# Linear attention and a mixture of experts on one core: the scanned decays go through DRAM, and 17 sets of prepared buffers become 19

## The chip, the core and the metric

The kernel runs on one core of a Trainium2 chip. A core has five engines that run side by side: TensorE (PE, matrix products, with a row of its own for weight loads, PEld), VectorE (DVE), ScalarE (ACT), GpSimd (POOL) and SyncE (SP, which here only issues transfers). Each works through its own list of instructions in order and waits where one needs a result that is not there yet; an instruction behind a waiting one waits too. Transfers are carried by 16 DMA engines that all issuing engines share. The metric is the device time of one execution in microseconds (us), less is better.

## The reference

Two computations follow each other, all in 32-bit floats. The first is a recurrence over 768 tokens for 4 batches and 8 heads of width 40:

```python
for t in range(S):
    y[:, :, t] = einsum('bhd,bhde->bhe', r_t, state)
    Sa = einsum('bhde,bhe->bhd', state, a_t)
    state = state * w_t[:, :, None, :] - einsum('bhd,bhe->bhde', Sa, b_t) + einsum('bhd,bhe->bhde', v_t, k_t)
```

The second takes the 3072 outputs `y` as rows of 320, forms gate logits `x @ w_gate`, balances their exponentials over rows and experts in 8 rounds, and sums over 8 experts `P[:, e] * (relu(x @ w1[e]) @ w2[e])`, with a hidden width of 1024.

## The kernel before

**The recurrence** is done in 12 chunks of 64 tokens (`c`), each for 4 batches (`b`): 48 steps in all, in the order of `c`, then `b`. Within a chunk the products of decays `w` are folded into `k`, `b`, `a` and the output, so that a chunk becomes a handful of small matrix products and the inverse of a triangular matrix. Three kinds of work make it up.

- A **preparation** (`prep`, lines 112 to 171, one for each `c, b`) needs only inputs. It loads them in one transfer (`inp`, line 115, 522 KB), scans the decays twice on VectorE (`q`, line 120, and `g`, line 128), multiplies `k` and `b` by `q` (`kb`, line 139) and `a` by `g` (`ab`, lines 145 and 146) on GpSimd, and forms four products `ll` and four transposes `kt` on TensorE (lines 151 and 159). What it leaves for the step later is a **set** of buffers: `sx`, `bb`, `cc` and `g`. There are `NSX` = 17 sets, used in rotation, so preparation n can write its set only when step n-17 is done with it. One part of `ll` goes to DRAM (`ld`, lines 154 and 170).
- An **inversion** (one for each pair of chunks, a segment, so six of them) starts when the eight preparations of the segment are done. It loads what they stored (`load_lu`, line 369), works on VectorE in 15 stages (`inv_diag`, `contract`, lines 173 to 223, about 24 us of VectorE time), ends with the copy `tn` (line 358), and stores two halves `ud` and `nd` to DRAM (lines 360 and 361). `tload` (lines 225 to 244) loads them back in another layout (`td`, `tt`), and `tmat` (lines 246 to 260: products `gp` and `op` on TensorE with copies on ScalarE between) makes of them the matrices `tt` of a chunk.
- A **step** (`recur`, lines 262 to 329) loads `v`, `r` and `vt` (lines 265 to 269), runs `av`, `xc`, `pu` (line 297, with `tt`) and `c2` on TensorE with masks and copies between them, adds up `ws` on VectorE, multiplies by `g` on GpSimd for the output `y` (line 308), stores `y` as `xd` (line 312), and hands the state `z` on. A step needs the state of the same batch one chunk before, so four of them overlap. Its gate products `lp` (line 334) follow a few steps later.

The program is written as a list of events with due times (lines 385 to 409): step (c, b) is due at 5c + 1.1b, preparation n just after step n - `NSX` at the earliest (line 399), an inversion after the last preparation of its segment. A scheduler then orders each engine's instructions by its own estimate of when they could run, with that list as priority. So `NSX` decides where preparations, and with them the inversions, stand among the steps.

**Memory.** The sets lie in pools of their own, in the order of last use (lines 33 and 50 to 63), and the second part's buffers (`stg`, `x0`, `hp`, `x1`, lines 477 to 495) take over their addresses when the first part lets go of them. Eight of the sets (`IN_SETS` and `KB_SETS`) are one raw tile, which the first preparations use for other things before it is a set.

**The experts** (lines 497 to 714) are split into 128 blocks; from block 8 the order of the work is written out by hand. Weights are loaded and split into a high and a low part on GpSimd and ScalarE ahead of use (`prep_w`, lines 497 to 528).

Of the kernel before, what the change touches and what calls it, by code (L numbers as in the profile page):

```python
# [11 lines left out]
F32 = mybir.dt.float32  # L12
F32R = mybir.dt.float32r
AF = mybir.ActivationFunctionType
ALU = mybir.AluOpType
# [5 lines left out]
NP = 4  # L21
R2 = 104
# [6 lines left out]
def attention(ctx, tc, d, xd, ps, pq, pt, gs, lg):  # L29
    nc = tc.nc  # L30
    pin = ctx.enter_context(tc.tile_pool(name="a_in", bufs=1))
    inv = ctx.enter_context(tc.tile_pool(name="a_inv", bufs=1))
    sets = [ctx.enter_context(tc.tile_pool(name=f"a_set{i}", bufs=1)) for i in range(NSX)]
    const = ctx.enter_context(tc.tile_pool(name="a_const", bufs=1))
    io = ctx.enter_context(tc.tile_pool(name="a_io", bufs=1))
    wk = ctx.enter_context(tc.tile_pool(name="a_wk", bufs=2))
    dr = ctx.enter_context(tc.tile_pool(name="a_dr", bufs=2, space=bass.MemoryType.DRAM))
# [7 lines left out]
    one65 = cst[0:R2, 400:660]  # L45

    NTB = 2
    sx_b, bb_b, g_b, cc_b = ([None] * NSX for _ in range(4))
    raws = {}
    for n in range(NCH * NB - NSX, NCH * NB):  # L50
        i, pool = n % NSX, sets[n - NCH * NB + NSX]
        if i in IN_SETS or i in KB_SETS:
            raw = pool.tile([128, 1508], F32, name=f"st{i}")
            raws[i] = raw
            sx_b[i] = raw[0:R2, 0:832].rearrange("r (p h x) -> r p h x", h=2, x=104)
            bb_b[i] = raw[:, 832:1248].rearrange("r (p x) -> r p x", x=104)
            g_b[i] = raw[0:R2, 1248:1504].rearrange("r (p x) -> r p x", x=64)
            cc_b[i] = raw[0:R2, 1504:1508]
            continue
        sx_b[i] = pool.tile([R2, NP, 2, 104], F32, name=f"sx{i}")  # L60
        bb_b[i] = pool.tile([128, NP, 104], F32, name=f"bb{i}")
        g_b[i] = pool.tile([R2, NP, 64], F32, name=f"g{i}")
        cc_b[i] = pool.tile([R2, NP], F32, name=f"cc{i}")
    tt_b = [const.tile([128, 4 * NP, 128], F32, name=f"tt{i}") for i in range(NTB)]
    td_b = [const.tile([128, 4 * NP, 32], F32, name="td")]
# [20 lines left out]
    def clear():  # L86
# [5 lines left out]
        for t in tt_b:  # L92
            nc.gpsimd.memset(t, 0.0)
    fresh = set(range(NSX))

    def first_use(i):
        if i in fresh:
            fresh.discard(i)
            nc.gpsimd.memset(bb_b[i], 0.0)
            nc.scalar.copy(out=sx_b[i][64:R2].rearrange("r p h x -> r (p h) x")[:, :, 64:104],  # L100
                           in_=cst[64:R2, 360:400].unsqueeze(1).broadcast_to([40, 8, 40]))
# [3 lines left out]
    def rot(key, lst):  # L105
        i = state[key]
        state[key] = (i + 1) % len(lst)
        return lst[i]
# [3 lines left out]
    def prep(c, b, ld):  # L112
        cb = c * NB + b
        inp = raws[IN_MAP[cb]][0:R2, 0:1284] if IN_MAP.get(cb) else pin.tile([R2, 1284], F32, name="inp", bufs=2)
        nc.sync.dma_start(out=inp, in_=d["inp"][c, b])
        w65 = inp[:, 0:516]
        kb_in = inp[:, 516:1028].rearrange("r (p k t) -> r p k t", p=NP, k=2)
        a_in = inp[:, 1028:1284].rearrange("r (p t) -> r p t", p=NP)
        q = pin.tile([R2, NP, 65], F32, name="q")
        nc.vector.tensor_tensor_scan(  # L120
            out=q.rearrange("r p t -> r (p t)"), data0=w65[:, 0:260], data1=one65,
            initial=0.0, op0=ALU.mult, op1=ALU.add)
        g1 = rot("g1", g1_b)
        nc.vector.reciprocal(out=g1[:, :, 0], in_=q[:, :, 64])
        sx = rot("sx", sx_b)
        i = next(j for j in range(NSX) if sx_b[j] is sx)
        g, bb, cc = g_b[i], bb_b[i], cc_b[i]
        nc.vector.tensor_tensor_scan(
            out=g.rearrange("r p t -> r (p t)"), data0=w65[:, 260:516],
            data1=g1.rearrange("r p t -> r (p t)"), initial=0.0, op0=ALU.mult, op1=ALU.add)  # L130
        if cb < NKB:
            raw = raws[KB_SETS[cb % len(KB_SETS)]]
            kb = raw[0:R2, 0:512].rearrange("r (p k t) -> r p k t", p=NP, k=2)
            lt = raw[0:64, 512:1024].rearrange("r (p k t) -> r p k t", p=NP, k=2)
        else:
            kb = pin.tile([R2, NP, 2, 64], F32, name="kb")
            lt = pin.tile([64, NP, 2, 64], F32, name="lt")
        eng = nc.vector if cb < NFAST else nc.gpsimd
        (nc.gpsimd if cb in KB_POOL else eng).tensor_tensor(
            out=kb, in0=kb_in,  # L140
            in1=q[:, :, 63::-1].unsqueeze(2).broadcast_to([R2, NP, 2, 64]), op=ALU.mult)
        ab = rot("ab", ab_b)
        first_use(i)
        nc.gpsimd.tensor_copy(out=cc, in_=q[:, :, 64])
        eng.tensor_tensor(out=ab[0:40, :, 0:64], in0=a_in[0:40], in1=g[0:40], op=ALU.mult)
        eng.tensor_tensor(out=ab[64:104, :, 64:128], in0=a_in[64:104], in1=g[64:104], op=ALU.mult)  # L146
        nc.scalar.copy(out=sx[64:104, :, 0, 0:64], in_=ab[0:40, :, 0:64])
        nc.scalar.copy(out=sx[64:104, :, 1, 0:64], in_=ab[64:104, :, 64:128])
        ll = pq.tile([128, NP, 2, 64], F32, name="ll", tag="pq")
        for p in range(NP):  # L150
            nc.tensor.matmul(ll[:, p], lhsT=kb[:, p], rhs=ab[:, p], start=True, stop=True)  # L151
        if cb < NKB:
            nc.scalar.activation(out=lt, in_=ll[64:128], func=AF.Copy, scale=-1.0)
            (nc.sync if cb < N_SP else nc.scalar).dma_start(out=ld[GRP[c][1], :, b], in_=lt)
            kt = pt.tile([128, NP, 2, 64], F32, name="kt", tag="pt")
        else:
            kt = pq.tile([128, NP, 2, 64], F32, name="kt", tag="pq")
        for p in range(NP):
            nc.tensor.transpose(kt[:, p].rearrange("s h x -> s (h x)")[:, 0:R2],
                                kb[:, p].rearrange("r k s -> r (k s)"), ident[0:R2, 0:R2])  # L160
        nc.vector.tensor_tensor(
            out=sx[0:64, :, :, 0:64], in0=ll[0:64],
            in1=mask_u.unsqueeze(1).unsqueeze(1).broadcast_to([64, NP, 2, 64]), op=ALU.mult)
        if cb >= NKB:
            nc.scalar.activation(out=lt, in_=ll[64:128], func=AF.Copy, scale=-1.0)
        nc.scalar.copy(out=sx[0:64, :, :, 64:104], in_=kt[0:64, :, :, 0:40])
        nc.scalar.activation(out=bb[0:64, :, 0:40], in_=kt[64:128, :, 0, 0:40], func=AF.Copy, scale=-1.0)
        nc.scalar.activation(out=bb[64:128, :, 64:104], in_=kt[64:128, :, 1, 0:40], func=AF.Copy, scale=-1.0)
        if cb >= NKB:
            (nc.sync if cb < N_SP else nc.scalar).dma_start(out=ld[GRP[c][1], :, b], in_=lt)  # L170
        return dict(cc=cc, g=g, sx=sx, bb=bb)

    def inv_diag(us, i):
        nu = us.stop - us.start
# [87 lines left out]
    def recur(c, b):  # L262
        pp = preps[c, b]
        vz, zc = vz_cur[b], zp[b]
        nc.sync.dma_start(out=vz[:, :, 0:64], in_=d["v"][c, b])
        rb = io.tile([R2, NP, 128], F32, name="rb", bufs=NRB)
        nc.sync.dma_start(out=rb, in_=d["r"][c, b])
        f = wk.tile([R2, NP, 2, 104], F32, name="f", bufs=NFB)
        nc.sync.dma_start(out=f[0:64].rearrange("s p h x -> s (p h) x")[:, :, 64:104],
                          in_=d["vt"][c, b].rearrange("s (g x) -> s g x", x=40))  # L270
# [6 lines left out]
        for p in range(NP):  # L277
            nc.tensor.matmul(av[:, p], lhsT=vz[:, p], rhs=rb[:, p], start=True, stop=True)  # L278
        nc.vector.tensor_tensor(
            out=f[:, :, :, 0:64], in0=av,  # L280
            in1=mask_f.unsqueeze(1).unsqueeze(1).broadcast_to([R2, NP, 2, 64]), op=ALU.mult)
# [14 lines left out]
        for p in range(NP):  # L296
# [3 lines left out]
                                op=ALU.mult)  # L300
# [4 lines left out]
        ws = wk.tile([R2, NP, 104], F32, name="ws")  # L305
        nc.vector.tensor_tensor(out=ws, in0=c2, in1=c1, op=ALU.add)
        y = wk.tile([R2, NP, 64], F32, name="y", bufs=NY)
        nc.gpsimd.tensor_tensor(out=y, in0=ws[:, :, 0:64], in1=pp["g"], op=ALU.mult)
        col = (b % 2) * 192 + (c % 3) * 64
        tok = (c // 3) * 768 + (col // 128) * 256 + (b // 2) * 128 + col % 128  # L310
        for h in range(2):
            nc.sync.dma_start(
                out=xd[h * 160:h * 160 + 160].rearrange("(p e) t -> e p t", e=40)[:, :, tok:tok + 64],
                in_=y[h * 64:h * 64 + 40])
        gq.append(gate(c, b, y))
        if c + 1 == NCH:
# [3 lines left out]
                                in1=preps[c + 1, b]["cc"].unsqueeze(2).broadcast_to([R2, NP, 40]), op=ALU.mult)  # L320
# [54 lines left out]
    def step(c, b):  # L375
        if (c, b) not in gens:
            gens[c, b] = recur(c, b)
        next(gens[c, b], None)

    def do_prep(s, c, b, first):  # L380
        if first:
            start_seg(s)
        preps[c, b] = prep(c, b, invs[s][0])
# [9 lines left out]
    for s, cs in enumerate(GROUPS):  # L393
# [3 lines left out]
        for i in range(n):  # L397
            cb = (cs[0] + i // NB, i % NB)
# [19 lines left out]
PD = 0.75  # L418
INV_DT = 0.05
SKEW = 1.1  # L420
NSX = 17
GL = 3
NY = 4
NFB = 3
# [2 lines left out]
IN_SETS = (16, 15, 14, 13)  # L427
# [409 lines left out]
```

## Time and profile before

| | us |
|---|---|
| median of 3 timed runs (lowest to highest) | 1893.79 (1890.14 to 1895.72) |
| the profiled execution's own time | 1882.69 |
| its span, first to last instruction | 1880.9 |
| TensorE busy, share of the span | 1774.0, 94% |
| mean granted TensorE clock | 0.945 |
| first `pu` of a step, last `pu` of a step | 108.58, 546.98 |

The profile is of one execution; times within it count from its first instruction. The recurrence fills roughly the first 555 us, the experts the rest, and they overlap a little at the seam. "Granted clock" is the share of full TensorE speed that the chip allowed at the time; read in windows of 10 us it lies between 0.50 and 1.00. "[4.47 <-DMA td<-nd]" behind a row means that the engine sat idle for 4.47 us before it and that this transfer ended the wait.

### The profile page before, as it was taken

The page shows a single profiled execution, that of the slowest core. Times are in us where ns is not written, and L with a number is a line of the kernel's source. Part 1 is how long each engine was busy: PE and PEld are TensorE (multiplying, and loading weights), DVE is VectorE, ACT ScalarE, POOL GpSimd, SP SyncE. Part 2 cuts the span into 40 slices and gives each one's busy share as a digit, 9 for nine tenths or more (in the row PEclk, how much of TensorE's full clock was granted, in tenths as well). Part 3 has the DMA queues.
Part 4 walks back from the last instruction along what each step waited for, and adds up shares of the span by engine and source line. Part 5 has one row for each costly group of instructions (what it writes and reads, how often), then busy time and mean ns, then how long its engine had stood idle before and what let it go on. Part 6 is the DMA issues. An engine that isn't in the chain of part 4 may idle for free.

```text
span 1880.9 us, 31865 instructions
## 1 busy us (share of the span) xinstructions
PE 1774.0 (94%) x12035; PEld 1733.0 (92%) x12035; DVE 1365.8 (73%) x2378; ACT 854.6 (45%) x1845; POOL 867.8 (46%) x846
## 2 busy tenths in 40 slices
PE   4489998899898999999999999999999999999999
PEld 4378887899788899999999999999999999999999
DVE  7865867848558867776777767886776867777676
ACT  6356667466543434343443434445343433434342
POOL 6545546331444345281744628004471826537170
PEclk8579989789689999999999999999999999999999
DMA  7578776685621111020111102111110201111011
GB/s 192 114 152 175 149 174 158 120 140 109 168 67 46 37 37 55 20 74 18 57 37 37 56 19 74 55 33 37 37 55 19 73 19 55 37 37 59 16 37 43
DMA packets 187839, 136.27 MB, mean 72 GB/s; under 512 B 155941, under 2 KB 165285, under 8 KB 187685
## 3 DMA queue, kind: packets, MB, share of 16 engines
q1 hardware_dynamic: 184485, 128.98, 27.7%
q10 hardware_dynamic: 3200, 5.25, 1.1%
q8 instruction: 95, 1.56, 0.4%
q14 instruction: 59, 0.48, 0.1%
HBM read 113.74 MB, written 20.45 MB: 71 GB/s over the span
## 4 chain that ended last, share of the span: by engine, by line
PE 78%; DVE 7%; DMA 7%; POOL 3%; issue 2%; ACT 2%; SPq 1%; ACTq 0%; POOLq 0%; DVEq 0%
PE op L637 35%; PE p L572 32%; DMA inp<-in_inp_dram 3%; PE xc L286 2%; PE pu L297 1%; PE ll L151 1%; PE av L278 1%; PE c L304 1%; PE lp L334 1%; DMA nd<-tn 1%; PE gp L253 1%; DVE pr L185 1%; DMA rb<-in_r_dram 1%; PE op L258 1%; POOL ab L146 1%
## 5 line engine op out<-in xcount | busy, mean ns | idle before, releaser
L572 PE MATMUL p<-xch,wh 128*128 128x384 f32 (+1 forms) x1792 | 605.6, 339 | 6.9 <-DVE u L590 2.4
L593 ACT ACTIVATE hh<-sm 128x384 fp32r<-128x384 f32 x512 | 269.4, 526 | 722.9 <-DVE sm L590 722.9
L637 PE MATMUL op<-wh,hh 128*128 128x320 f32 x1536 | 477.8, 312 | 2.9 <-ACT hh L593 2.8
L637 PE MATMUL op<-wl,hh 128*128 128x320 f32 x1536 | 475.6, 310 | 0.0
L637 PE MATMUL op<-wh,hl 128*128 128x320 f32 x1536 | 468.8, 311 | 2.4 <-DVE hl L596 2.4
L518 POOL TENSOR_TENSOR wl<-ws,wh 128x640 fp32r<-128x640 f32 x60 | 103.3, 1721 | 608.7 <-ACT wh L516 608.5
L596 DVE SCALAR_TENSOR_TENSOR hl<-sm,hh 128x384 fp32r<-128x384 f32 x512 | 368.0, 752 | 2.2 <-ACT hh L593 2.0
L572 PEld LDWEIGHTS p<-xch,wh 128*128 128x128 f32 (+1 forms) x1792 | 337.8, 189 | 10.4 <-DVE u L590 4.1
L572 PE MATMUL p<-xcl,wh 128*128 128x384 f32 x896 | 302.9, 338 | 0.0
L572 PE MATMUL p<-xch,wl 128*128 128x384 f32 x896 | 302.3, 337 | 0.0
L637 PEld LDWEIGHTS op<-wh,hh 128*128 128x128 f32 x1536 | 291.1, 189 | 3.7 <-ACT hh L593 3.7
L637 PEld LDWEIGHTS op<-wl,hh 128*128 128x128 f32 x1536 | 291.6, 190 | 0.0
L637 PEld LDWEIGHTS op<-wh,hl 128*128 128x128 f32 x1536 | 287.6, 188 | 3.2 <-DVE hl L596 3.1
L590 DVE TENSOR_TENSOR sm<-p,u 128x384 f32<-128x384 f32 x384 | 234.8, 621 | 8.8
L572 PEld LDWEIGHTS p<-xcl,wh 128*128 128x128 f32 x896 | 168.9, 188 | 0.0
L572 PEld LDWEIGHTS p<-xch,wl 128*128 128x128 f32 x896 | 168.8, 188 | 0.0
L590 DVE TENSOR_TENSOR sm<-p,p 128x384 f32<-128x384 f32 x128 | 71.3, 557 | 129.7 <-PE p L572 76.9
L590 DVE TENSOR_TENSOR p<-p,p 128x384 f32<-128x384 f32 x128 | 71.2, 556 | 103.6 <-PE p L572 101.6
L590 DVE TENSOR_TENSOR u<-p,p 128x384 f32<-128x384 f32 x128 | 70.8, 553 | 59.8 <-PE p L572 58.7
L526 POOL TENSOR_TENSOR wl<-ss,wh 128x512 fp32r<-128x512 f32 x60 | 90.8, 1514 | 35.3 <-ACT wh L523 31.2
L151 PE MATMUL ll<-ab,kb 104*128 104x128 f32 x336 | 63.7, 349 | 45.9 <-POOL ab L146 21.8
L151 PEld LDWEIGHTS ll<-ab,kb 104*128 104x128 f32 x336 | 55.5, 250 | 50.7 <-POOL ab L146 30.2
(166 smaller groups left out, 2793.9 us busy)
## 6 DMA issues: line engine op xcount, KB each, us to landing
ws<-in_wts_dram SPq DMA_DIRECT2D x60, 832.0 KB
inp<-in_inp_dram SPq DMA_DIRECT2D x42, 521.6 KB
rb<-in_r_dram SPq DMA_DIRECT2D x48, 208.0 KB
ld<-lt ACTq DMA_DIRECT2D x40, 128.0 KB
vz<-in_v_dram SPq DMA_DIRECT2D x48, 104.0 KB
f<-in_vt_dram SPq DMA_DIRECT2D x48, 80.0 KB
xd<-y SPq DMA_DIRECT2D x96, 40.0 KB
st<-in_inp_dram SPq DMA_DIRECT2D x6, 521.6 KB
```

The source lines that it names most:

```text
L146: eng.tensor_tensor(out=ab[64:104, :, 64:128], in0=a_in[64:104], in1=g[64:104], op=ALU.mult)
L151: nc.tensor.matmul(ll[:, p], lhsT=kb[:, p], rhs=ab[:, p], start=True, stop=True)
L185: nc.vector.tensor_tensor(out=prv, in0=a.unsqueeze(2).broadcast_to([nu, n_c, n_r, n_k]), in1=m.unsqueeze(1).broadcast_to([nu, n_c, n_r, n_ ...
L253: nc.tensor.matmul(gp[:, p], lhsT=lb[:, p], rhs=t1[:, p], start=True, stop=True)
L286: nc.tensor.matmul(xc[h][:, p], lhsT=pp["sx"][:, p, h], rhs=f[:, p, h], start=True, stop=True)
L518: g.tensor_tensor(out=wl[:, 0:640], in0=raw[:, 256:896], in1=wh[:, 0:640], op=ALU.subtract)
L526: g.tensor_tensor(out=lv[:, 3:7], in0=so[:, :, 0], in1=hv[:, 3:7, 0], op=ALU.subtract)
L572: nc.tensor.matmul(o, lhsT=w_, rhs=x_, start=(j == 0), stop=(j == 3))
L590: eng.tensor_tensor(out=out, in0=x, in1=y, op=ALU.add)
L593: nc.scalar.activation(out=hh[:, f, h], in_=sm[f][:, h], func=AF.Relu)
L596: v.scalar_tensor_tensor(out=hl[:, f, h], in0=sm[f][:, h], scalar=0.0, in1=hh[:, f, h], op0=ALU.max, op1=ALU.subtract)
L637: nc.tensor.matmul(ops[i], lhsT=a[:, h, cs], rhs=w_[:, cw], start=(f == 0 and h == 0 and j == 0), stop=(last and h == 1 and j == 2))
```

## The change

`g` is no longer part of a set. The preparation scans it into a buffer of two that turn (`g`, in the pool of the preparations) and stores it to a DRAM tile of its own (`gd`, 104 KB); the step loads it into another buffer of two (`gl`) for the product `y`. Both transfers are issued on SP. A set is smaller by about 1 KB in each partition, and `NSX` is 19.

```diff
-    sx_b, bb_b, g_b, cc_b = ([None] * NSX for _ in range(4))
+    sx_b, bb_b, cc_b = ([None] * NSX for _ in range(3))
...
-            raw = pool.tile([128, 1508], F32, name=f"st{i}")
+            raw = pool.tile([128, 1284 if i in IN_SETS else 1252], F32, name=f"st{i}")
...
-            g_b[i] = raw[0:R2, 1248:1504].rearrange("r (p x) -> r p x", x=64)
-            cc_b[i] = raw[0:R2, 1504:1508]
+            cc_b[i] = raw[0:R2, 1248:1252]
...
-        g_b[i] = pool.tile([R2, NP, 64], F32, name=f"g{i}")
...
-        g, bb, cc = g_b[i], bb_b[i], cc_b[i]
+        bb, cc = bb_b[i], cc_b[i]
+        g = pin.tile([R2, NP, 64], F32, name="g", bufs=2)
         nc.vector.tensor_tensor_scan(
             out=g.rearrange("r p t -> r (p t)"), data0=w65[:, 260:516],
             data1=g1.rearrange("r p t -> r (p t)"), initial=0.0, op0=ALU.mult, op1=ALU.add)
+        gd = dr.tile([R2, NP, 64], F32, name=f"gd{cb}", bufs=1)
+        nc.sync.dma_start(out=gd, in_=g)
...
-        return dict(cc=cc, g=g, sx=sx, bb=bb)
+        return dict(cc=cc, g=gd, sx=sx, bb=bb)
...
+        gl = io.tile([R2, NP, 64], F32, name="gl", bufs=2)
+        nc.sync.dma_start(out=gl, in_=pp["g"])
...
-        nc.gpsimd.tensor_tensor(out=y, in0=ws[:, :, 0:64], in1=pp["g"], op=ALU.mult)
+        nc.gpsimd.tensor_tensor(out=y, in0=ws[:, :, 0:64], in1=gl, op=ALU.mult)
...
-NSX = 17
+NSX = 19
```

The scheduler moves instructions on every engine; line numbers of the recurrence are up to three higher in the changed kernel. Three places show what moved. In the rows, `A<-B,C` is what an instruction writes and reads.

The first place is VectorE at the end of the last inversion, that of chunks 10 and 11. `pm` (line 299 before, 302 after) stands once in each step; `tn<-un` is the inversion's last operation. Before:

```order
L299 TENSOR_TENSOR pm<-pu,cst 128x416
L319 TENSOR_TENSOR z<-ws,cc_180 104x160
L185 TENSOR_TENSOR pr<-gt,tn 128x1024
L279 TENSOR_TENSOR f<-av,cst 104x8x64
L188 TENSOR_REDUCE un<-pr 128x8x8
L306 TENSOR_TENSOR ws<-c_4949,c_202 104x416
L299 TENSOR_TENSOR pm<-pu,cst 128x416
L358 COPY tn<-un 128x16x16
```

Up to that copy `pm` has stood 40 times, so it comes behind the `pm` of the last step of chunk 9, and the next step is the first that needs its result. The same place after:

```order
L302 TENSOR_TENSOR pm<-pu,cst 128x416
L186 TENSOR_TENSOR pr<-gt,tn 128x1024
L322 TENSOR_TENSOR z<-ws,cc_173 104x160
L189 TENSOR_REDUCE un<-pr 128x8x8
L342 COPY lg<-lp 64x8
L282 TENSOR_TENSOR f<-av,cst 104x8x64
L361 COPY tn<-un 128x16x16
```

Here `pm` has stood 38 times: the inversion ends two steps earlier in the list. For the inversions of the second to the fifth segment (first needed by steps 8, 16, 24 and 32) the count moves from 6 to 4, from 15 to 14, from 24 to 22 and from 27 to 30; for the first it is 0 in both.

The second place is TensorE where the preparations at the start end and the first chunk's matrices are made (`gp`, `op`) ahead of the first step's `pu`. Before, the list goes from the seventeenth preparation's products to `gp`:

```order
L151 MATMUL ll<-ab_194,kb 128x128 x4
L159 MATMUL kt<-cst,kb 128x104 x4
L253 MATMUL gp<-td,lg 64x32 x8
L258 MATMUL op<-td,lg 64x32 x8
L253 MATMUL gp<-td,lg 64x32 x8
L297 MATMUL pu<-x_881,tt_190 128x104 x4
```

After, one more preparation stands ahead of them:

```order
L152 MATMUL ll<-ab_197,kb 128x128 x4
L160 MATMUL kt<-cst,kb 128x104 x4
L152 MATMUL ll<-ab_198,kb 128x128 x4
L160 MATMUL kt<-cst,kb 128x104 x4
L254 MATMUL gp<-td,lg 64x32 x8
L259 MATMUL op<-td,lg 64x32 x8
L254 MATMUL gp<-td,lg 64x32 x8
L300 MATMUL pu<-x_934,tt_193 128x104 x4
```

So 18 preparations, not 17, are ahead of the first step; later the lead is mostly 17 preparations, where it was mostly 16.

The third place is SP behind the last inversion: the stores of `ud` and `nd`, the loads of `td` and `tt` that wait for them, and the output's stores `xd`. Before:

```order
L360 DMA ud<-un 64x1024 x2
L361 DMA nd<-tn 64x1024 x2
L240 DMA td<-ud 32x16x32 x2
L238 DMA td<-nd 32x16x32 x2
L244 DMA tt_190<-ud 32x16x32 x4
L312 DMA xd<-y 40x4x64 x2
```

After, a load of the decays and a step's output stand between the stores and the loads:

```order
L363 DMA ud<-un 64x1024
L364 DMA nd<-tn 64x1024
L363 DMA ud<-un 64x1024
L364 DMA nd<-tn 64x1024
L270 DMA gl<-gd_3418 104x256
L315 DMA xd<-y 40x4x64 x2
L239 DMA td<-nd 32x16x32 x2
L241 DMA td<-ud 32x16x32 x2
L245 DMA tt_193<-ud 32x16x32 x4
```

The load `gl` takes the buffer that a step two earlier has used, so it waits for that step's `y`, as `xd` does. It stands directly ahead of an `xd` in all steps but the first ones, and a store `gd` stands between many of them.

## The prediction

> **What bounds the kernel now.** I read the busy time by stage first. Columns: stage, its length, busy us of TensorE, its weight loads, VectorE, ScalarE and GpSimd, then granted clock, share of the DMA engines, GB/s.
>
> ```profile
> 0.00:100.00 100.00, 44.60 (x226) 39.96 (x227) 76.93 (x134) 48.97 (x120) 61.56 (x87) 0.67 0.70 160
> 100.00:310.00 210.00, 195.15 (x1791) 181.52 (x1791) 154.32 (x283) 137.88 (x349) 108.61 (x127) 0.91 0.77 157
> 310.00:420.00 110.00, 98.46 (x779) 90.95 (x778) 71.09 (x121) 63.70 (x161) 45.70 (x59) 0.78 0.73 140
> 420.00:463.00 43.00, 43.00 (x443) 40.19 (x443) 34.11 (x66) 25.53 (x65) 8.29 (x12) 1.00 0.46 93
> 463.00:560.00 97.00, 86.48 (x650) 79.17 (x647) 48.76 (x87) 48.42 (x107) 39.09 (x40) 0.77 0.46 117
> 660.00:1881.00 1221.00, 1216.75 (x7639) 1215.65 (x7637) 895.69 (x1524) 488.41 (x962) 559.22 (x482) 1.00 0.13 42
> ```
>
> From 660 on TensorE is full at full clock, and the change doesn't touch that part. Everything is decided before 560: TensorE bounds there too, but it loses time twice, in waits and in half clock. From 420 to 463, where it never waits, its clock is whole. So the question is which waits go, and what clock comes with them.
>
> Next the timeline of TensorE, the line `pu` that stands once in each step (start, duration, row):
>
> ```profile
> 237.66 1.06 PE L297 MATMUL pu<-x,tt 128*128 128x104 f32 x8
> 254.09 2.04 PE L297 MATMUL pu<-x,tt 128*128 128x104 f32 x8
> 262.58 0.83 PE L297 MATMUL pu<-x,tt 128*128 128x104 f32 x6
> ...
> 314.38 1.63 PE L297 MATMUL pu<-x,tt 128*128 128x104 f32 x8
> 331.75 2.04 PE L297 MATMUL pu<-x,tt 128*128 128x104 f32 x8
> 344.72 1.06 PE L297 MATMUL pu<-x,tt 128*128 128x104 f32 x8
> ...
> 419.24 1.06 PE L297 MATMUL pu<-x,tt 128*128 128x104 f32 x8
> ...
> 463.80 1.06 PE L297 MATMUL pu<-x,tt 128*128 128x104 f32 x8
> 478.43 2.04 PE L297 MATMUL pu<-x,tt 128*128 128x104 f32 x8
> 491.07 1.67 PE L297 MATMUL pu<-x,tt 128*128 128x104 f32 x8
> ```
>
> These are steps 15, 16, 17, 23, 24, 25, 32, 39, 40 and 41, counted from 0. Steps 17 to 23 take (314.38 - 262.58)/6 = 8.63 us each, beside preparations; steps 32 to 39, with none, (463.80 - 419.24)/7 = 6.37. Against that the first steps on a new inversion come late: 15 to 16 takes 16.43, 23 to 24 17.37 and the next 12.97, 39 to 40 14.63 and the next 12.64. The chain of waits tells what holds step 40:
>
> ```profile
> 466.14 0.62 DVE tn L358
> 466.79 3.42 DMA nd<-tn
> ...
> 470.62 2.17 DMA td<-nd
> 472.92 1.90 PE gp L253 x16
> ...
> 475.63 1.91 PE op L258 x16
> ...
> 478.50 1.97 PE pu L297 x8
> ```
>
> From the inversion's last copy to the step's `pu` are 478.50 - 466.14 = 12.4 us of transfers and small products, which nothing covers, since that copy stands right behind step 39's `pm` on VectorE. The same waits, as TensorE sees them, with the clock around two of them (windows of 10 us):
>
> ```profile
> 246.00 1.40 PE L253 MATMUL gp<-td,lg 64*64 64x32 f32 x16 [1.75 <-DMA td<-nd]
> 326.25 1.88 PE L253 MATMUL gp<-td,lg 64*64 64x32 f32 x16 [1.78 <-DMA td<-nd]
> 472.92 1.88 PE L253 MATMUL gp<-td,lg 64*64 64x32 f32 x16 [4.47 <-DMA td<-nd]
> ```
>
> ```profile
> 250.00:260.00 10.00, 9.75 (x64) 9.54 (x64) 3.20 (x9) 4.36 (x11) 3.90 (x6) 0.50 0.81 171
> 480.00:490.00 10.00, 10.00 (x57) 8.79 (x56) 1.69 (x4) 2.79 (x7) 2.81 (x4) 0.50 1.01 286
> ```
>
> After each of the two, TensorE is busy for ten us at half clock.
>
> **The change part by part: the gain.** Excess over the undisturbed pace: 16.43 - 8.63 = 7.8 at step 16; 8.7 and 4.3 at steps 24 and 25; 14.63 - 6.37 = 8.3 and 6.3 at steps 40 and 41; together 35.4 us. In the new order the three inversions end one, two and two steps earlier. One step is 8.6 us against the 7.8 at step 16, two are 17.3 against 8.7, and two late ones 12.7 against the chain's 12.4, so by length all could close. Bounds: 0 and 35.4. I take half, 17.7, for two reasons: a step that no longer waits for its matrices finds its other inputs just in time, and the SP list now has `gl`, `xd` and often a `gd` between an inversion's stores and the loads of `td`, so part of the lead is spent in that queue. The fifth inversion ends later in the list (27 to 30), but still two steps ahead of step 32; I count nothing for it.
>
> The rule that speaks about the clock: the Trainium skill, page "TensorE: Matmul & The Clock Gate", section "Why this matters for your kernels", wants no gaps on TensorE over about 3 us, since one idle window halves the clock. By it only the 4.47 us wait would cost clock, the gross gain would be 1.75 + 1.78 + 8.3 + 6.3 = 18.1, half of it 9.1, and the sum -9.1 + 8.7 = -0.4, which the second rival below reaches from rows alone. The trace is against that limit: behind the wait of 1.75 us the clock is 0.50 from 250 to 260.
>
> **The start.** One more preparation stands ahead of the first `gp`:
>
> ```profile
> 93.47 2.08 PE L151 MATMUL ll<-ab,kb 104*128 104x128 f32 x8 [4.77 <-POOL ab L146]
> ...
> 99.58 2.08 PE L151 MATMUL ll<-ab,kb 104*128 104x128 f32 x8 [3.34 <-POOL ab L146]
> ...
> 102.69 1.91 PE L253 MATMUL gp<-td,lg 64*64 64x32 f32 x16 [0.33 <-DMA td<-nd]
> ```
>
> Preparations come 99.58 - 93.47 = 6.1 us apart there, paced by GpSimd, and `gp` has nothing to spare. So the first step starts 6.1 later; the preparation is missing later, where steps with one differ from steps without by 8.63 - 6.37 = 2.3. Net +3.8 (bounds 0, if `gp`'s wait grows by other means anyway, and 6.1).
>
> **The transfers.** 48 stores and 48 loads of 104 KB, 2 x 106.5 KB = 213 KB a step. The rows nearest to them, from SP's timeline (shortest/median/longest ns to issue one), SP's waits (us in total, times, longest), the chain, and a stage:
>
> ```profile
> L265 SPq DMA_DIRECT2D vz<-in_v_dram x48: 816/868/4757, 4.4 to 490.4; - x48
> L267 SPq DMA_DIRECT2D rb<-in_r_dram x48: 308/338/1006, 5.5 to 520.8; - x48
> SPq L312 <- POOL y L308: 82.7, 27, 7.8
> 28.11 5.61 DMA ld<-st
> ...
> 46.46 2.44 DMA ld<-lt
> 375.00:410.00 35.00, 33.70 (x252) 31.43 (x253) 15.76 (x30) 20.81 (x53) 14.07 (x22) 0.76 0.96 165
> ```
>
> Issuing one takes SP 0.34 (`rb`, contiguous rows) to 0.87 us (`vz`); I take 0.34, so 33 us for 96. SP sits 82.7 us in waits for `y` alone (27 times, 7.8 at most), which hides it: 0. The loads are not waited for: `gl` is issued two steps, 12.7 us or more, ahead of its `y`, and a store of 128 KB lands in 2.44 to 5.61. The two `g` buffers: a scan waits until the store two preparations back has landed; queued 7.8 behind a `y`, landing in 5.61, that is 13.4 against two steps, 17.3. At the start the preparations are 6.1 apart and no `y` is waited for: 5.61 against 12.2. So 0; without that cover it is VectorE that stands, with every step's masks behind it. On the DMA engines the bytes take, at 157 GB/s for a 0.77 share (204 at a whole one), 1.04 us a step. It counts where they are full: 375 to 410 at 0.96 are four steps; doubling that for shorter full stretches gives 9 us at most, 0 at least. I take 4.
>
> **The sets.** Two more first uses cost GpSimd a memset each at the start:
>
> ```profile
> L99 POOL MEMSET bb<- 128x416 f32 x9 | 3.6, 445 | 0.3 <-POOLq L826 0.3
> ```
>
> 2 x 0.445 = +0.9 (0 if it falls into GpSimd's waits). The smaller set, the new layout and the seam to the experts: at the last `y` the GpSimd list goes on with the same pieces of weight preparation in both orders, so 0.
>
> **Sum**: -17.7 + 3.8 + 4 + 0.9 = -9.0. The profiled execution would go from a span of 1880.9 (1882.69 with what lies around it) to 1871.9. It was 11.1 faster than the median of the timed runs; taken off that median, 1893.79 - 9.0 = **1884.8**. Its own range, with the gain between a third and three quarters of 35.4 (11.8 to 26.6) less 8.7, is 1876 to 1891.
>
> **The rivals.** *All of the excess goes.* For it speaks the length of the lead; against it, that the SP list gave part away. -35.4 + 8.7 = -26.7: 1867.1.
>
> *The waits go, the clock doesn't come back.* From 375 to 410 the clock is 0.76 with TensorE busy 33.7 of 35 us and no inversion due: short waits elsewhere keep it low. Then only the idle time is won, 1.75 + 1.78 + 4.47 = 8.0, against 8.7: 1894.5, no change. A lead that the steps don't need looks the same. The page's limit on gaps would end near here.
>
> *Slower: the loads of the inverse wait in SP's queue.* With `gl` and `xd` ahead of them, `td` and `tt` are issued only when a `y` is done, and where a `gd` stands there too, when VectorE has scanned. If that takes the two steps that the inversion is earlier, `gp` comes when it came, the gain is 0 and the costs stay: +8.7, 1902.5 (with each at its upper bound, 6.1 + 9 + 0.9, 1909.8). It decides once SP waits there for more than 17.3 - 12.4 = 4.9 us between steps with preparations, or 0.3 in the late ones; its mean wait for `y` is 82.7/27 = 3.1. Against it: `td` has to wait 3.42 for the store anyway, and most `y` are done by then.
>
> **How the numbers follow.** A measurement of this kernel tells about 0.3%, 5.7 us, from no change: 1888.1 to 1899.5 counts as the same. Chances: forecast 0.46, all of it 0.10, clock stays 0.19, slower by SP 0.25. Faster: 0.38 of the forecast, 0.10, and 0.02 of the third case = 0.50. Same: 0.08 + 0.14 + 0.03 (forecast, third, last) = 0.25. Slower: 0.03 of the third and 0.22 of the last = 0.25. The range leaves out the better half of the first rival and the upper end of the last: 1869 to 1905.
>
> **What would show it.** Right: `pu` of steps 16, 24 and 40 within 10 us of the one before, no wait for `td` over 1 us at `gp`, a clock near 0.9 from 310 to 420 and 463 to 500; the first `pu` near 115; a DMA share up by some 0.05. Wrong: `gp` still released by `td` with `td` issued more than 5 us after the store landed (SP), VectorE waiting for `gd` ahead of a scan (buffers), or the same clock with fewer waits.

## The result and the profile after

| | before | after |
|---|---|---|
| median of 8 timed executions each, us | 1894.76 | 1871.66 |
| lowest to highest, us | 1887.99 to 1913.22 | 1866.00 to 1883.61 |
| the profiled execution, us (span) | 1882.69 (1880.9) | 1880.34 (1878.6) |
| a second profile, of experiments 1 and 5 (span) | 1888.45 (1886.7) | 1879.56 (1877.8) |
| TensorE idle in the two profiles, us | 106.9, 105.1 | 109.1, 99.4 |
| mean granted clock of the timed executions | 0.939 (of 23, with experiment 5) | 0.952 |

The ratio of after to before is **0.988, 95% interval 0.984 to 0.991**: faster, by 23 us of medians. The profiled execution of before was one of its quickest, and that of after one of its slowest; so the two profiles differ by 2.3 us and the second pair by 8.9, and what a profile shows is where time moved more than how much was won.

The timeline of TensorE after, the `pu` of steps 15, 16, 23, 24, 25, 39, 40 and 41, and ahead of step 40's the `gp` that makes its matrices:

```profile
269.04 1.04 PE L300 MATMUL pu<-x,tt 128*128 128x104 f32 x8
278.14 1.06 PE L300 MATMUL pu<-x,tt 128*128 128x104 f32 x8
...
349.65 1.06 PE L300 MATMUL pu<-x,tt 128*128 128x104 f32 x8
356.95 1.14 PE L300 MATMUL pu<-x,tt 128*128 128x104 f32 x8
...
367.04 1.06 PE L300 MATMUL pu<-x,tt 128*128 128x104 f32 x8
...
479.24 1.06 PE L300 MATMUL pu<-x,tt 128*128 128x104 f32 x8
482.73 1.08 PE L254 MATMUL gp<-td,lg 64*64 64x32 f32 x16 [0.53 <-DMA td<-nd]
488.00 1.14 PE L300 MATMUL pu<-x,tt 128*128 128x104 f32 x8
...
493.56 1.06 PE L300 MATMUL pu<-x,tt 128*128 128x104 f32 x8
```

The gaps are 9.1 (16.4 before), 7.3 (17.4), 10.1 (13.0), 8.8 (14.6) and 5.6 (12.6). Over the paces of 8.63 and 6.37 that is 0.5 + 0 + 1.5 + 2.4 + 0 = 4.4 us of excess, where it was 35.4. The three steps behind them gained too: from step 41 to 44 it takes 23.4 us, before 34.5. The wait for `td` at step 40 is 0.53 us, where it was 4.47. The clock in that place, in windows of 10 us, and then the stages (columns as in the prediction):

```profile
470.00:480.00 10.00, 10.00 (x98) 9.47 (x98) 5.56 (x12) 6.45 (x17) 0.87 (x1) 1.00 0.63 162
480.00:490.00 10.00, 9.13 (x107) 8.67 (x107) 3.47 (x9) 5.34 (x15) 1.59 (x2) 1.00 0.67 138
490.00:500.00 10.00, 10.00 (x109) 9.41 (x108) 2.95 (x6) 6.94 (x18) 0.87 (x1) 1.00 0.67 121
```

```profile
0.00:100.00 100.00, 44.02 (x212) 39.31 (x212) 69.02 (x125) 46.48 (x114) 55.01 (x83) 0.68 0.72 162
100.00:310.00 210.00, 185.50 (x1580) 172.63 (x1580) 150.78 (x270) 124.96 (x315) 96.55 (x121) 0.82 0.81 168
310.00:420.00 110.00, 104.85 (x886) 96.67 (x884) 80.12 (x138) 71.20 (x181) 57.00 (x69) 0.84 0.81 170
420.00:463.00 43.00, 41.12 (x405) 38.15 (x405) 29.08 (x58) 25.52 (x65) 8.30 (x14) 0.96 0.68 142
463.00:560.00 97.00, 90.18 (x807) 83.62 (x805) 60.83 (x102) 59.71 (x132) 40.29 (x43) 0.89 0.56 144
660.00:1878.00 1218.00, 1214.55 (x7632) 1213.63 (x7631) 893.43 (x1523) 487.15 (x960) 557.30 (x481) 1.00 0.13 42
```

From 480 to 490 the clock is 1.00, where it was 0.50. By stage it rises from 0.78 to 0.84 and from 0.77 to 0.89 where the late inversions were. It falls from 0.91 to 0.82 from 100 to 310, a stretch that now begins with the end of the start: the first `pu` stands at 124.04 and not at 108.58. The share of the DMA engines is up by 0.04 to 0.22 in the four stages from 100 to 560.

The start is the other thing that moved. The first two `ll` before stand at 10.13 and

```profile
15.00 2.08 PE L151 MATMUL ll<-ab,st 104*128 104x128 f32 x8 [0.95 <-DVE ab L146]
```

After, the second one comes 9.9 us later. TensorE's rows (`ll`, then the first `gp` and `pu`), SP's issues and VectorE's scans after:

```profile
24.86 1.91 PE L152 MATMUL ll<-ab,st 104*128 104x128 f32 x8
...
116.95 1.89 PE L254 MATMUL gp<-td,lg 64*64 64x32 f32 x16 [1.29 <-DMA td<-ud]
...
124.04 2.03 PE L300 MATMUL pu<-x,tt 128*128 128x104 f32 x8
```

```profile
10.08 5.58 SPq L266 DMA_DIRECT2D vz<-in_v_dram  x1
15.71 1.19 SPq L268 DMA_DIRECT2D rb<-in_r_dram  x1
16.94 1.97 SPq L272 DMA_DIRECT2D f<-in_vt_dram  x1
19.02 2.20 SPq L131 DMA_DIRECT2D gd<-g  x1
```

```profile
25.52 0.69 DVE L127 TENSOR_TENSOR_SCAN g<-st,g 104x256 f32<-104x256 f32 x1 [7.23 <-DMA gd<-g]
...
31.23 0.69 DVE L127 TENSOR_TENSOR_SCAN g<-st,g 104x256 f32<-104x256 f32 x1 [2.07 <-DMA gd<-g]
```

The first store `gd` is issued only at 19.02, behind three loads for the first steps that SP takes 8.9 us to issue. The third scan needs the buffer of the first, so VectorE stands 7.23 us with everything behind it: the wait that the prediction priced at 0. The view of waits has all of it, VectorE from 0 to 125 (us in total, times, longest):

```profile
DVE g L127 <- DMA gd<-g: 10.5, 4, 7.2
DVE lu L193 <- DMA lu<-ld: 5.6, 1, 5.6
```

From the positions of `pu` the profiles add up as follows: the first step 15.5 later, steps 0 to 47 in 421.7 us and not 438.4 (-16.7), the rest behind the last `pu` 1.1 shorter, -2.3 in all. The second pair: +14.9, -19.5 and -4.3, -8.9 in all.

### The profile page after: what moved, and what is told of

The parts are those of the page before. It is cut to its first block, busy times and chain, and to the rows that moved or that the text cites. A ratio compares the mean times of both kernels' runs of the same rounds, so it can differ in the third digit from the quotient of the medians.

```text
span 1878.6 us, 32050 instructions
## 1 busy us (share of the span) xinstructions
PE 1769.5 (94%) x12035; PEld 1728.9 (92%) x12035; DVE 1368.1 (73%) x2378; ACT 856.6 (46%) x1847; POOL 860.1 (46%) x848
## 3 DMA queue, kind: packets, MB, share of 16 engines
q1 hardware_dynamic: 195717, 139.21, 29.7%
## 4 chain that ended last, share of the span: by engine, by line
PE 79%; DVE 7%; DMA 6%; issue 2%; POOL 2%; SPq 1%; ACT 1%; DVEq 0%; POOLq 0%; ACTq 0%
PE op L640 35%; PE p L575 33%; DMA inp<-in_inp_dram 3%; PE xc L289 2%; PE ll L152 1%; PE pu L300 1%; PE c L307 1%; PE av L281 1%; PE lp L337 1%; DMA ld<-lt 1%; PE op L259 1%; DVE q L118 1%; PE gp L254 1%; DVE pr L186 1%; DMA gl<-gd 1%
## 5 line engine op out<-in xcount | busy, mean ns | idle before, releaser
L575 PE MATMUL p<-xch,wh 128*128 128x384 f32 (+1 forms) x1792 | 605.4, 339 | 10.3 <-DVE mxs L661 3.3
L311 POOL TENSOR_TENSOR y<-ws,gl 104x256 f32<-104x256 f32 x48 | 42.9, 894 | 138.1 <-DVE ws L309 99.8
```

The lines of the kernel that those rows point to most:

```text
L311: nc.gpsimd.tensor_tensor(out=y, in0=ws[:, :, 0:64], in1=gl, op=ALU.mult)
L575: nc.tensor.matmul(o, lhsT=w_, rhs=x_, start=(j == 0), stop=(j == 3))
```

## The experiments

Theories: **O** says that the gain comes from the order, that is, from the inversions ending some two steps ahead of their use in VectorE's list. **S** says that it takes the two more sets. The rest of the questions are the start and the price of the transfers. Ratios are to the kernel before, run beside each; brackets are 95% intervals.

### 1 and 5: both kernels once more

The changed kernel as it is, five rounds:

> The changed kernel once more, for a second profile and a time beside the others on the same chip. Every theory: ratio to before 0.984 to 0.992, about 1872 us; first pu of a step near 124 where before had 108.6, and no step on a new inversion more than 10 us behind the one before it.

1876.31 us (1867.13 to 1883.91), ratio 0.990 [0.986, 0.994]; first `pu` at 123.8, the gaps to steps 16, 24, 25, 40 and 41 13.2, 7.3, 6.2, 8.9 and 5.6. The kernel before, a second profile:

> The kernel before, a second profile of it, since the first was the fastest of its executions by some 11 us. Every theory expects the same places: gaps between pu of 14 to 18 us at steps 15 to 16, 23 to 24 and 39 to 40, a first pu near 109 us, and a time of 1884 to 1912.

1888.45 us; first `pu` at 109.0, gaps to steps 16, 24 and 40 of 16.2, 17.2 and 14.2. Both pictures repeat; only step 16 after varies (9.1, and 13.2 against the 10 that were expected at most).

### 2: the decays in DRAM, with 17 sets

```diff
-NSX = 19
+NSX = 17
```

> The changed kernel with 17 sets: decays through DRAM, no additional set. Theory S (two more sets let preparations and inversions run ahead): the gain is lost and the costs stay, ratio 1.000 to 1.008, 1895 to 1910 us. Theory O (what counts is that the inversions end two steps ahead in the VectorE list, and a set without g is free as soon as c2 is done, which gives that with 17 sets too; the list has the ends at steps 6, 14, 22, 30, 39 where the changed kernel has 4, 14, 22, 30, 38): ratio 0.986 to 0.993, 1870 to 1881 us.

1883.52 us, 0.992 [0.989, 0.995]. Without the two sets most of the gain is there. The inversions end behind 0, 6, 14, 22, 30 and 39 `pm`: already better than before (15, 24, 40 at the third, fourth and sixth). In the code a set without `g` is done with when `c2` has read it and doesn't wait for `y`; that this moves the scheduler's estimate is argued, not shown. So S falls as the whole cause.

### 3: 19 sets, but preparations due as with 17

```diff
-            j = cb[0] * NB + cb[1] - NSX
+            j = cb[0] * NB + cb[1] - 17
```

> 19 sets, but line 402 gives the preparations the due times that they have with 17. Theory S with the list as its lever: the preparations come no earlier, ratio 0.998 to 1.005, 1890 to 1903 us. Theory O: the inversions still end at 6, 14, 22, 31, 37 in the list, ratio 0.985 to 0.993; with 17 preparations, not 18, ahead of the first step its pu comes some 6 us earlier than in the changed kernel, near 118.

1886.53 us, 0.994 [0.991, 0.998], between the ranges of the two theories. The inversions end behind 0, 6, 14, 22, 31 and 37. The fifth, first needed by step 32, is now one step ahead of it, and there a wait at `gp` is back, on TensorE:

```profile
417.66 1.09 PE L254 MATMUL gp<-td,lg 64*64 64x32 f32 x16 [1.72 <-DMA td<-nd]
```

The gaps to steps 32 to 36 are 13.1, 12.6, 11.4, 11.1 and 10.3 us, where the change has 6 to 8. So one step of lead brings O's wait back in a new place. Most of the loss is clock: in the four windows of 10 us from 420 to 460 TensorE is busy throughout, at 0.50, 0.67, 0.50 and 0.50. Why the clock stays low for so long isn't shown: in experiment 4 the same `gp`, with two steps of lead, waits about as long, and there the clock is back at 0.88 from 430 to 440.

```profile
416.40 1.09 PE L254 MATMUL gp<-td,lg 64*64 64x32 f32 x16 [1.89 <-DMA td<-nd]
```

### 4: the store of the decays issued on ScalarE

```diff
-        nc.sync.dma_start(out=gd, in_=g)
+        nc.scalar.dma_start(out=gd, in_=g)
```

> The store of the decays is issued by ScalarE, not SP. If the 15 us by which the first pu comes later are lost in SP's queue (lu loads behind gd stores), the first pu comes back to 110 to 116 and the time falls by 8 to 14 us below the changed kernel, about 1860. If they are lost to the added preparation and the two g buffers, the first pu stays within 3 us of 124 and the time within 5 us of the changed kernel.

1870.74 us, 0.988 [0.984, 0.992], as the change. The wait for `gd` leaves VectorE's list of waits at the start, and another takes its place, with the first `pu` at 127.4:

```profile
DVE sx L162 <- ACT st L154: 13.7, 4, 9.4
```

Now ScalarE stands behind the issue of the stores, and VectorE behind ScalarE. So issuing the store elsewhere isn't the remedy. The first store doesn't even leave earlier: ScalarE, idle since 9.05, issues it at 18.70, where SP issued it at 19.02.

```profile
18.70 0.59 ACTq L131 DMA_DIRECT2D gd<-g  x1
19.32 0.40 ACT L148 COPY sx<-ab 40x256 f32<-40x256 f32 x1 [10.28 <-DMA inp<-in_inp_dram]
```

The profile lays ScalarE's wait to a load of inputs. So the three loads ahead of the store in SP's list are not what holds it, or not alone; what does stays open.

### 6 and 8: the inversions due earlier still

One line ahead of the loop over `INV` moves the inversions of the second to the sixth segment up by one step's due time, in the kernel before (6), and in the changed one with four buffers for `g` (8):

```diff
         ev.append((t, load_lu, (s, len(cs))))
+        t -= 1 if s else 0
         for i, (fn, a) in enumerate(INV):
```

> The kernel before, 17 sets with the decays in them and nothing in DRAM; one line more lowers the due time of the inversions of the second to the sixth segment by 1, so that in VectorE's list they end behind 4, 10, 17, 24 and 31 pm, not 6, 15, 24, 27 and 40. Theory O (what counts is where the inversions stand in the list): the gaps at steps 16, 24 and 40 close to 10 us or less, the first pu stays near 109, and as neither the start nor the transfers cost anything the ratio is better than that of the change: 0.981 to 0.987 of the time before (1858 to 1872). Theory S (two more sets let the preparations, and so the inversions, run ahead): with 17 sets the inversion would wait for the same late preparations, the gaps stay, 0.997 to 1.003. A rival to both: an inversion that stands among the steps delays their masks, 0.99 to 1.0.

> The changed kernel with four buffers for the decays and with the inversions of the second to the sixth segment due 1 earlier, so that they end behind 4, 10, 17, 23 and 30 pm. Theory O and the start's wait together: no gap at steps 8, 16, 24, 32, 40, first pu at 110 to 117, ratio 0.978 to 0.984. If the change has all that the order can give, the same as with four buffers alone, within 3 us.

6 gives 1885.05 us, 0.9945 [0.991, 0.998]; 8 gives 0.991 [0.988, 0.994], worse than four buffers alone (below). O had both at 0.978 to 0.987, and misses both. The order alone, in 6, gives about half of what the change gives. Its first `pu` doesn't stay near 109 either, though no decay is moved and no preparation more stands ahead of it:

```profile
114.51 2.03 PE L297 MATMUL pu<-x,tt 128*128 128x104 f32 x8
```

The inversions of the second to the sixth segment now end four to nine steps ahead of use, and behind the start no `gp` waits for `td` any more. But step 24 comes 20.3 us after step 23, and step 32 18.4 after step 31. VectorE, then TensorE, then the windows at step 24:

```profile
326.55 0.70 DVE L120 TENSOR_TENSOR_SCAN q<-inp,cst 104x260 f32<-104x260 f32 x1 [3.02 <-DMA inp<-in_inp_dram]
```

```profile
330.53 1.16 PE L151 MATMUL ll<-ab,kb 104*128 104x128 f32 x8 [2.37 <-POOL ab L146]
```

```profile
320.00:330.00 10.00, 8.16 (x86) 7.48 (x83) 6.98 (x11) 6.47 (x18) 5.20 (x6) 1.00 0.76 181
330.00:340.00 10.00, 9.47 (x49) 8.23 (x50) 4.71 (x10) 6.30 (x16) 5.21 (x7) 0.58 0.84 205
340.00:350.00 10.00, 10.00 (x66) 9.49 (x64) 3.87 (x8) 2.83 (x8) 3.03 (x5) 0.57 0.55 119
```

A preparation waits for its inputs, the steps stand behind it, and 20 us at 0.58 of the clock follow. So O holds in part: an inversion that ends at the last moment costs, but once it is well ahead the next late thing, here a preparation's load, takes its place, and the lead that this line adds doesn't pay.

### 7 and 9: four buffers for the scanned decays

```diff
-        g = pin.tile([R2, NP, 64], F32, name="g", bufs=2)
+        g = pin.tile([R2, NP, 64], F32, name="g", bufs=4)
```

> The changed kernel with four turning buffers for the scanned decays, not two. If the late start (first pu at 124 and not 109) is the second scan's wait for the first store, it goes: VectorE waits for no gd in the first 125 us, the first pu comes at 110 to 117, and the ratio to the kernel before is 0.980 to 0.986 (6 to 12 us less than the change). Rival: the next late thing at the start takes its place (the loads, the one more preparation, the four products' copies on ScalarE), first pu at 121 or later and the time within 3 us of the change's.

> The changed kernel with four buffers for the scanned decays, a second time: ratio 0.980 to 0.988 if its first value, 0.9839, holds; the same as the change, 0.988 to 0.991, if it was chance. First pu at 119.

1866.53 us, **0.984 [0.980, 0.988]**, and again 1866.85, **0.983 [0.978, 0.987]**: the best of all kernels here, ahead of before in both, and 5 to 10 us below the change's two medians (taken on other chips; the intervals of the ratios overlap). In experiment 7 `gd` is gone from VectorE's waits at the start, of which the longest are now

```profile
DVE lu L193 <- DMA lu<-ld: 6.0, 1, 6.0
DVE q L118 <- POOL kb L140: 5.9, 4, 3.3
DVE lu L193 <- DMA td<-nd: 5.1, 1, 5.1
```

and the first `gp` moves from 116.95 to

```profile
111.95 1.88 PE L254 MATMUL gp<-td,lg 64*64 64x32 f32 x16 [1.29 <-DMA td<-nd]
```

The first `pu` comes at 119.0 and 119.4, 4.5 to 5.0 us earlier than with two buffers, not the 7 to 14 that were expected: of VectorE's 10.5 us about half was worth time.

### 10: four buffers with 17 sets

```diff
-NSX = 19
+NSX = 17
```

> The decays in DRAM with four buffers, but 17 sets: the two kernels differ in NSX alone, and neither has the wait for gd. 17 preparations stand ahead of the first gp, not 18, and inversions end behind 0, 6, 14, 22, 29 and 39 pm, not 0, 4, 14, 22, 30 and 38. Theory O (what the change wins comes by the order that follows from keeping the decays outside the sets): 0.981 to 0.988, within 0.3% of four buffers with 19 sets, and a first pu at 113 to 116. Theory S (the two more sets are worth something of their own): 0.3% or more slower than with 19 sets, 0.988 to 0.994, with gaps over 12 us at steps 40 and 41, where the last inversion ends one step later.

1877.29 us, 0.986 [0.983, 0.990], against 1866.85 and 0.983 [0.978, 0.987] for 19 sets on the same chip: between the two forecasts. The gaps over 12 us that S expected at steps 40 and 41 are not there (9.1 and 8.5). With one preparation fewer ahead of `gp` the first `pu` comes at 115.1, 4.3 earlier. Later the matrices of step 16 wait for `td`, and the steps take longer (424 us from first to last `pu`, 411 with 19 sets):

```profile
249.29 1.08 PE L254 MATMUL gp<-td,lg 64*64 64x32 f32 x16 [1.96 <-DMA td<-nd]
```

Here and between experiments 1 and 2 the two sets look worth 0.2 to 0.4%, both times within the uncertainty: S as a second, smaller cause stays open. What 19 sets do without DRAM wasn't tried, since they don't fit.

### 11 and 12: the transfers made twice

With four buffers, each store and each load of decays a second time; the second load goes to the same tile (11) or to one of its own (12):

```diff
         nc.sync.dma_start(out=gd, in_=g)
+        nc.sync.dma_start(out=dr.tile([R2, NP, 64], F32, name=f"ge{cb}", bufs=1), in_=g)
...
+        gm = io.tile([R2, NP, 64], F32, name="gm", bufs=1)
+        nc.sync.dma_start(out=gm, in_=pp["g"])
         nc.sync.dma_start(out=gl, in_=pp["g"])
```

> Four buffers and 19 sets, and each of the 96 transfers of decays is made twice (the second store goes to a tile that nobody reads): 213 KB more a step. The inversions end behind 0, 4, 12, 21, 28 and 37 pm, so the lead is as good. If the transfers cost what was forecast, 4 us for the pair, the time is 2 to 6 us above the one with single transfers (0.986 to 0.988); if they are free, within 2 us of it (0.983 to 0.985); if the DMA engines are what bounds the stretches with preparations, 9 us or more (0.989 and up) and a share of the DMA engines of 0.9 from 100 to 420.

> As the kernel that moves each transfer of decays twice, but the second load goes to a tile of its own, so that SP does not wait for the first load to land; inversions end behind 0, 5, 12, 21, 29 and 37 pm. If the 61 us of that kernel came from SP standing in its list (57.5 us of waits of the second load for the first), they go, and what is left is the price of the bytes and of two more issues a step: 0.985 to 0.992 of the kernel before, 4 to 15 us above the single transfers (1866.85). If the bytes themselves cost that much, because the DMA engines bound the stretches with preparations, it stays at 1.00 or above, with the share of the DMA engines near 0.9 from 100 to 420.

11 gives 1927.68 us, 1.015 [1.011, 1.020]; 12 gives 1909.48, 1.009 [1.006, 1.013]: slower than before. 12 is 43 us above single transfers by medians, which were taken on different chips, and by ratios 1.009 less the mean of 0.984 and 0.983, 0.026 of 1895, so 49 us. In 11 SP stands 57.5 us for the first load ahead of the second:

```profile
SPq L272 <- DMA gl<-gd: 57.5, 38, 3.4
```

In 12 a third of that is left, since `gm` has one buffer and a load into it can wait for the one before:

```profile
SPq L272 <- DMA gm<-gd: 19.2, 13, 2.9
```

From 11 to 12 the time falls by 18 us by medians, 11 by ratios (whose intervals overlap). The rest, 43 to 49 us, is the price of 96 more transfers with their issues and these waits; the runs don't separate bytes from queue. Stages of the kernel of experiment 9, then of 12:

```profile
100.00:310.00 210.00, 191.59 (x1596) 178.53 (x1596) 148.67 (x272) 127.13 (x322) 102.88 (x122) 0.80 0.80 170
310.00:420.00 110.00, 99.86 (x967) 91.91 (x965) 75.57 (x136) 76.50 (x194) 54.95 (x67) 0.96 0.89 180
```

```profile
100.00:310.00 210.00, 178.66 (x1502) 166.50 (x1503) 149.31 (x265) 121.55 (x306) 101.37 (x116) 0.80 0.85 179
310.00:420.00 110.00, 101.86 (x880) 95.33 (x878) 80.53 (x138) 68.99 (x175) 61.80 (x70) 0.84 0.86 185
```

The share of the DMA engines goes from 0.80 to 0.85 in the longer stage and from 0.89 to 0.86 in the shorter one: a little short of the 0.9 by which the expectation wanted to know full engines. TensorE is busy 13 us less in the longer one. In 12 the first `pu` is 10.3 later than in 9, steps 0 to 47 take 29.7 longer and the rest 6.7. On TensorE `gp` waits for `td` again, though the inversions end behind 5, 12, 21, 29 and 37 `pm`:

```profile
123.76 1.91 PE L255 MATMUL gp<-td,lg 64*64 64x32 f32 x16 [3.71 <-DMA td<-nd]
...
381.51 1.25 PE L255 MATMUL gp<-td,lg 64*64 64x32 f32 x10 [4.08 <-DMA td<-ud]
...
500.20 1.88 PE L255 MATMUL gp<-td,lg 64*64 64x32 f32 x16 [3.51 <-DMA td<-nd]
```

The order moves a little with every edit too: experiments 3 and 1, or 10 and 9, whose lists differ about as much, are 10 us apart, and 43 is well outside that.

## Why the prediction was right, and where it was not

The forecast was 1884.8 in a range of 1869 to 1905; 1871.66 lies near the range's lower end, and the gain of 23 us is more than twice the 9.0 of the sum. The sign and the place of the gain are shown; two terms had the wrong size, in opposite directions, so that the range held in part by luck. Of the signs named for being right, the gaps, the waits at `gp` and the clock came true (1.00 from 463 to 500, 0.84 from 310 to 420), the first `pu` near 115 did not, and one named for being wrong came too: VectorE waits for `gd` ahead of a scan.

- **The late inversions** were a loss, and the new order takes it away. Of the 35.4 us of excess at steps 16, 24, 25, 40 and 41, 31 are gone in the profile after, not the 17.7 that were counted. Experiment 3, which brings one inversion back to one step, brings its wait back with it. Some is given back elsewhere: steps 9 to 10 take 15.7 (9.3 before), 21 to 22 16.3 (11.2), 44 to 45 14.3 (6.2), and steps 0 to 15 together 145.0 (129.1). The reason given for halving the gain, SP's queue between the stores and `td`, did not show: no `gp` behind the start waits over 0.53 us for `td` (0.64 in the second profile). So the rival with SP falls for this kernel.
- **The gain's size.** Taking 17.7 for five gaps that gave 31 was the step that failed. By profile, steps 0 to 47 gained 16.7 and 19.5 net, where the terms -17.7 - 2.3 + 4 make 16.0; that these agree is luck, since the 14 us that the other steps gave back on balance had no term. And the timed executions gained 23.1 and 19.4 over all; if the start was 15 us worse in them too, the steps and the rest must have gained some 34 to 39. The profiles of after don't show all of that; they were taken at a clock of 0.945 and 0.939, the timed executions at 0.952 and 0.947 on the mean.
- **The clock.** The rival in which the clock doesn't come back is refuted in its place (1.00 for 0.50 from 480 to 490) and by the time, which isn't its 1894.5. Over the whole span the profiles of a pair have about the same clock (0.945 and 0.945, 0.941 and 0.939), since the stage from 100 to 310 lost what the others won; in the timed executions it rises. TensorE's idle time is about the same in all four profiles (105 to 107 before, 99 to 109 after): what the late inversions lost in waits is now lost early, with 9.7 us more idle time from 100 to 310. The busy time times the clock is 1774.0 x 0.945 = 1676 us of full clock in the first profile; from 0.939 to 0.952 that shrinks by 1676/0.939 - 1676/0.952 = 24 us, about what the medians differ by. But these two clocks were not taken side by side; in experiment 1, where they were, the clock rises from 0.939 to 0.9465, which makes 14 of the 19.4 us. That waits moved into a start where the clock is low anyway (0.68 from 0 to 100) is a reading of this; no run isolates it.
- **The start** was forecast 6.1 + 0.9 later and came 15.5 later. The term that failed is the wait for the two `g` buffers, priced at 0 with "5.61 against 12.2": the landing was compared and not the issue, which came 9.7 us after the first scan was done. The prediction's own row of `vz` has such an issue as its longest (4757 ns, at 9.63 us in the kernel before); the sum went by the short ones. But the three loads on SP are not the whole cause, since ScalarE issues the store no earlier (experiment 4). The wait's price is 4.5 to 5.0 us (experiments 7 and 9). The preparation more, priced 6.1, measures 4.3 with four buffers (10 against 9) and 2.4 to 2.6 with two (2 against 1 and the change). Some 6 us are left, with the first `pu` at 115.1 against 109 even then. Doubled transfers move it by 10.3, but experiment 6, which moves no decays, is 5.5 to 5.9 us late too, at 114.51. So a changed order alone can do it, and the transfers are not shown to be the cause.
- **The transfers**, 4 us in a range of 0 to 9, are the least certain term. The first dose can't be taken away without changing the rest; the second costs 43 to 49, issues and waits included. The bound of 9 came from the bytes in stretches with full engines; the waits that later transfers bring, such as the 3.5 to 4.1 us at `gp` in experiment 12, were not in it. What the first dose costs is still open; it is inside the net gain. It doesn't by itself explain the 145.0 us of steps 0 to 15: experiment 10 makes all of these transfers and takes 129.7 there (129.1 and 130.7 before), and experiment 6 makes none and takes 140.3.
- **The sets.** Experiment 2 shows that most of the gain needs no additional set, and experiment 6 that the order alone gives 0.5%; where the rest comes from, and the worth of two more sets, 0.2 to 0.4%, isn't settled.

## What to carry to other kernels

When work is rotated through few buffers, a new transfer out of them needs the time from when the data is ready to when it is issued, not only its landing; count that at the start of the program, where the first loads are still under way, and give it more buffers there (here two more brought the first step 4.5 to 5.0 us forward, and the ratio from 0.988 and 0.990 to 0.984 and 0.983). A serial piece that ends just before its use can cost its whole latency and the clock behind it. One step of lead was too little here (step 16 before, step 32 in experiment 3), two were mostly enough, but not in experiment 4; beyond that the next late thing decides. Price added traffic by doubling it on the chip: where the DMA engines are at 0.8, transfers that look free by their duration may not be.

## What the runs showed of the hardware

A `vz` issue that takes SP 0.87 us in the median took 5.58 us at 10.08 us (4.76 at 9.63 in the kernel before), and in that time nothing else leaves SP; what held it the trace doesn't show. A wait of TensorE of 2.37 us was followed by a clock of 0.58 and 0.57 in the next two windows of 10 us (experiment 6). The Trainium skill, page "TensorE: Matmul & The Clock Gate", section "Why this matters for your kernels", wants gaps over about 3 us avoided; by these rows the limit is too wide for this kernel, as the wait of 1.75 us before the change said already. Not every short wait costs clock: one of 1.65 us, in the second profile of the change, ended at 422.78, and the clock was 1.00 in the 10 us behind it.
